# First chunk's gate moved behind the second chunk's step two, q loaded ahead of w_mod and half of it asked for by GpSimd, in a kernel of FFT convolution and token mixer

## The chip, the cores and the metric

The kernel runs on one core of a Trainium2 chip. The metric is the device time of one execution in microseconds (us), the median of several runs. Beside the runs, one execution was recorded by the profiler; its trace gives start and length of each instruction on the five engines: PE (TensorE matmul; PEld is its weight load), DVE (VectorE), ACT (ScalarE), POOL (GpSimd) and SP (SyncE, which here only asks for DMA transfers). A queue that asks for transfers is marked SPq or ACTq.

## The reference

Sequence 2048 (S), channels 640 (D), hidden size 1728 (F), all in float32:

```python
    mod = (_silu(c) @ w_mod).reshape(c.shape[0], 6, 1, -1)
    sa, ca, ga, sb, cb, gb = (mod[:, 0], mod[:, 1], mod[:, 2], mod[:, 3], mod[:, 4], mod[:, 5])
    h = _layernorm(x, axis=-1) * (1 + ca) + sa
    x = x + ga * _A_ref(h, A_k, A_v, A_shift_k, A_ssm_k, A_ssm_D)
    h = _layernorm(x, axis=-1) * (1 + cb) + sb
    x = x + gb * _B_ref(h, B_w1, B_b1, B_w2, B_b2)
```

with x = q at the start. `_A_ref` shifts k by a causal filter of four taps per channel, multiplies it by v (kv), convolves kv along the sequence with `ssm_k` per channel (by FFT), adds kv times `ssm_D`, and multiplies the result by h: the gate. `_B_ref` is an MLP over the sequence axis: layer norm, w1, gelu, w2. So h, the left factor of the gate, needs the layer norm of all of q and three of the six rows of mod; the convolution needs neither.

## The kernel before

The part that the change touches is the first block, `_A_ref`. It goes over five chunks of 128 channels (`NC = 5`, loop over `c` at L511). A chunk's convolution is a DFT in two steps each way, all of it matmuls on PE:

- kv (`kv_ops`, L171): four groups `g` of eight operations on DVE, or on POOL (its own scratch), from KX and VX (k and v of the chunk, in the tile `in`) into X, the tile `x`. The taps come from `rows` into TAP (PSUM) or PW.
- `ssm_k` is loaded into KSR, the lower half of the tile `aux` (`load_ks`, L149); POOL or DVE adds `ssm_D` (`perm_add`), ACT rearranges it into KSP, the tile `p` (`perm`).
- step one (`step1(side, t)`, L210): four blocks for X (side 0), four for KSP (side 1), each 16 matmuls into a PSUM buffer, evacuated by ACT into Z.
- step two (`f2(g)`, L223): eight blocks; 32 matmuls, ACT copies one half into kt, DVE multiplies twice into `p` (`mul`), POOL or DVE adds into `y` (`add`). `mul` of block g needs the half of `p` that `add` of block g - 2 has read.
- the way back (`i2`, L254, two halves; `i1`, L273, two halves): `i2` takes two PSUM buffers each, `i1` one.
- the gate (`gate`, L299): DVE multiplies A1 by the PSUM of `i1`, POOL adds the product to q in `xa` or `xb`; `spill` writes the chunk to DRAM. A1 is the upper half of `aux`: 16 rows of the normalized q by ACT (`a1_ops`, L286), times G1 and plus G0 by DVE.

PSUM has a ring of three buffers for all these steps and a fourth, `tap`, for taps and the sums of mod. The order is written by hand (the program is emitted in the order in which the engines run it); each engine goes through its instructions in that order, and so does each queue of DMA requests. While chunk c goes through step two, the kv work of a later chunk fills DVE's gaps (`fill`, taken by `dv(n)`).

The start and the first pass differ from the others. Chunk 0's kv is made before the loop, then chunk 1's, into the same X once PE has read it. SP's queue then holds w2 (the constants of step two), four bias loads into `g`, taps of chunk 2, q in 32 transfers of 64 rows (L494 to L496: for each of 16 `j`, the lower and the upper 64 partitions), and four of five parts of w_mod, two of which lie in the place of v1 (the constants of the way back) and two in `aux`. The mod rows come from five `mod_part`s on PE into `tap` (L338), `mod_sum`, and three `mod_row`s, which make G0 and G1 with ACT and DVE (L349).

In pass 0, after step two: 16 rows of statistics of q on DVE (L540 to L543), step one of chunk 1's kv, the `mod_part`s among `i2`, v1 and chunk 1's `ssm_k` only once parts of w_mod have been used, `rstd`, A1, chunk 2's kv group 2 on POOL, then `i1`, the gate of chunk 0, and step one of chunk 1's `ssm_k`. Then pass 1 begins with step two.

## Time and profile before

| what | value |
|---|---|
| runs | 696.41, 697.76, 707.59 us; median 697.76 |
| the profiled execution | 697.86 us, its span 696.1 us |
| mean granted PE clock | 0.975 of full |
| PE busy | 622.0 us, 89% of the span |
| DVE, ACT, POOL busy | 496.1, 291.6, 128.2 us |
| moved by DMA | 84.37 MB, 121 GB/s over the span |
| step two of chunks 1, 2, 3 begins on PE | 115.45, 164.87, 209.23 us |

The span runs from the first to the last instruction; what the time has beyond it lies around the program. The profile's page lists busy time by engine, the span in 40 slices, the DMA queues, the chain of work that ended last (followed back from the end, at each step to what released it), and the costliest groups of instructions. The timeline gives start and length of single instructions or runs of them, with the idle time before in brackets and what ended it. Names of tiles stand as out<-in; L59 is the line of the helper TT, so DVE's and POOL's elementwise work is told apart by its tiles. The times of an issue on SPq are those of the request, not of the data.

### The profile page before, as it was taken

To read this page: it belongs to the slowest core of one execution; us is meant where nothing else is said; L and a number is where in the kernel's file an instruction comes from. 1 tells how busy PE (TensorE), PEld (TensorE's weight loads), DVE (VectorE), ACT (ScalarE), POOL (GpSimd) and SP (SyncE) were. 2 spreads that over 40 slices of the span, in tenths; PEclk is the share of its full clock that TensorE was granted. 3 is DMA by queue.
4 is the path that set the end of the run, shared out by engine and by line. 5 is a ranking of instruction groups with operands and counts; after the bars stand their busy time and mean duration, and the time that the engine had idled before them with its cause. 6 is when DMAs were issued, how large, how long until landed. Compare 5 with 4: busy or idle time off the path is not lost.

```text
span 696.1 us, 20691 instructions
## 1 busy us (share of the span) xinstructions
PE 622.0 (89%) x9099; PEld 595.8 (86%) x9099; DVE 496.1 (71%) x866; ACT 291.6 (42%) x464; POOL 128.2 (18%) x147
## 2 busy tenths in 40 slices
PE   0689777898998988888899999999999989999997
PEld 0688466788988888778899979999999989999997
DVE  6769448978979449888985741123499868888986
ACT  0444373554746536456666232232244233233331
POOL 5184018513425025000100000000000430000000
PEclk9999798999999999999999999999999999999999
DMA  9988988627443424171305604433353533466611
GB/s 183 243 227 232 381 169 178 145 43 155 91 79 111 145 64 121 59 153 32 60 1 91 121 2 99 84 61 64 110 141 104 167 121 99 121 173 172 167 44 38
DMA packets 166930, 84.37 MB, mean 121 GB/s; under 512 B 91030, under 2 KB 157368, under 8 KB 166840
## 3 DMA queue, kind: packets, MB, share of 16 engines
q1 hardware_dynamic: 162292, 81.74, 46.9%
q10 hardware_dynamic: 4548, 1.31, 1.1%
q8 instruction: 71, 1.16, 0.7%
q14 instruction: 19, 0.16, 0.1%
HBM read 72.55 MB, written 10.49 MB: 119 GB/s over the span
## 4 chain that ended last, share of the span: by engine, by line
PE 62%; DVE 17%; DMA 6%; ACT 5%; SPq 4%; issue 3%; POOL 1%; ACTq 0%; POOLq 0%; DVEq 0%
PE pst L436 20%; PE pst L997 17%; PE pst L1074 7%; PE pst L218 5%; PE pst L233 4%; PE pst L262 4%; SPq L496 3%; DVE tap L59 3%; PE pst L282 2%; DVE p L59 2%; DMA aux<-in_A_ssm_k_dram 2%; DVE kt L59 2%; DMA w<-in_const_w_dram 1%; DMA aux<-in_w_mod_dram 1%; DVE aux L59 1%
## 5 line engine op out<-in xcount | busy, mean ns | idle before, releaser
L233 PE MATMUL pst<-z,w 128*64 128x64 f32 x2560 | 79.0, 223 | 12.0 <-ACT z L220 5.7
L233 PEld LDWEIGHTS pst<-z,w 128*64 128x64 f32 x2560 | 76.8, 138 | 14.8 <-issue 7.7
L220 ACT ACTIVATE z<-pst 128x1024 f32<-128x1024 f32 x40 | 43.0, 1076 | 51.4 <-PE pst L218 51.3
L218 PE MATMUL pst<-v,x 128*64 128x128 f32 x640 | 39.6, 282 | 27.2 <-DVE x L59 24.1
L218 PEld LDWEIGHTS pst<-v,x 128*64 128x64 f32 x640 | 36.9, 142 | 28.1 <-POOL t L459 23.6
L59 DVE TENSOR_TENSOR p<-pst,kt 128x512 f32<-128x512 f32 x80 | 50.9, 680 | 12.7 <-ACT kt L237 9.3
L59 POOL TENSOR_TENSOR y<-p 128x256 f32<-128x256 f32 x72 | 51.1, 744 | 38.8 <-DVE p L59 38.6
L218 PE MATMUL pst<-v,p 128*64 128x128 f32 x640 | 39.7, 283 | 6.8 <-DVE aux L59 4.6
L997 PE MATMUL pst<-r_z,m_w 128*128 128x320 f32 x222 | 42.1, 312 | 2.2 <-DVE m_w L59 2.2
L218 PEld LDWEIGHTS pst<-v,p 128*64 128x64 f32 x640 | 37.2, 143 | 8.0 <-DVE aux L59 4.9
L262 PEld LDWEIGHTS pst<-v,y 32*128 32x128 f32 x1280 | 39.7, 194 | 3.8 <-issue 2.6
L237 ACT ACTIVATE kt<-pst 128x512 f32<-128x512 f32 x40 | 23.9, 599 | 43.7 <-PE pst L233 30.1
L262 PE MATMUL pst<-v,y 32*128 32x64 f32 x1280 | 41.6, 279 | 0.7 <-ACT z L220 0.6
L833 ACT ACTIVATE pst<-pst,sm 128x640 f32<-128x640 f32 x13 | 10.0, 767 | 75.8 <-PE pst L436 75.8
L985 ACT ACTIVATE m_w<-m_v 128x896 fp32r<-128x896 f32 x24 | 22.7, 951 | 37.0 <-PE pst L997 16.8
L997 PEld LDWEIGHTS pst<-r_z,m_w 128*128 128x128 f32 x222 | 35.2, 190 | 2.4 <-DVE m_w L59 2.4
L59 DVE TENSOR_TENSOR tap<-tap,kt 128x512 f32<-128x512 f32 x51 | 35.5, 696 | 1.3
L59 DVE TENSOR_TENSOR kt<-in,tap 128x512 f32<-128x512 f32 x51 | 34.9, 685 | 1.4
L59 POOL TENSOR_TENSOR m_p<-u_i,r_z 128x320 f32<-128x320 f32 x1 | 0.9, 882 | 183.4 <-issue 183.4
L271 ACT ACTIVATE z<-pst 128x512 f32<-128x512 f32 x38 | 20.9, 646 | 21.9 <-PE pst L262 21.9
L59 DVE TENSOR_TENSOR m_w<-m_v,m_w 128x896 fp32r<-128x896 f32 x24 | 27.9, 1164 | 2.4 <-ACT m_w L985 1.9
L436 PE MATMUL pst<-r_z,wb0b 128*128 128x320 f32 x180 | 28.2, 310 | 0.9 <-DVE u_x L59 0.9
(289 smaller groups left out, 1445.0 us busy)
## 6 DMA issues: line engine op xcount, KB each, us to landing
x<-in_B_w_dram SPq DMA_DIRECT2D x20, 512.0 KB
aux<-in_A_ssm_k_dram SPq DMA_DIRECT2D x10, 512.0 KB
in<-in_A_k_dram SPq DMA_DIRECT2D x36, 128.0 KB
in<-in_A_v_dram SPq DMA_DIRECT2D x36, 128.0 KB
m_x<-xs SPq DMA_DIRECT2D x28, 160.0 KB
out_dram<-m_x SPq DMA_DIRECT2D x28, 160.0 KB
w<-in_const_w_dram SPq DMA_DIRECT2D x2, 2048.0 KB
m_v<-in_B_w_dram SPq DMA_DIRECT2D x9, 448.0 KB
```

The costliest lines, as they stand in the source:

```text
L59: TT = lambda eng, o, a, b, op: eng.tensor_tensor(o, a, b, op=op)
L218: pe.matmul(ps[64 * ri:64 * ri + 64, o:o + 255:2], lhs, F1[:, 128 * ri:128 * ri + 128], start=True, stop=True)
L220: evac = lambda: act.activation(Z[:, side, t], ps.rearrange("p (a k e) -> p a k e", a=4, e=2), AF.Copy)
L233: pe.matmul(ps[64 * h:64 * h + 64, o:o + 64], W2[k1 // 32][:, 2 * (k1 % 32) + ri], rhs, start=True, stop=True)
L237: act.activation(kt.rearrange("p (m i) -> p m i", i=32), pv[:, :, 1], AF.Copy)
L262: pe.matmul(pp[qd // 2][:, o:o + 64], Y[p, ri, i:i + 2].rearrange("p i k -> p (i k)"), V2[p, 64 * ri:64 * ri + 64], start=ri == 0, stop=ri ...
L271: act.activation(o, i, AF.Copy)
L436: pe.matmul(ps[0:m, h, 0:320], w_.bitcast(F32R), r_[:, 320 * h:320 * h + 320].bitcast(F32R), start=first and i == 0, stop=last and i == 2)
L496: sync.dma_start(XH[j // 8][64 * b:64 * b + 64, j % 8], dram(q, (16 * b + j) * D, [[32 * D, 64], [1, D]]))
L985: act.activation(W[n][0].bitcast(F32R), A[p, w_], AF.Copy)
L997: pe.matmul(bank[n], w[:, i].bitcast(F32R), r.bitcast(F32R), start=i == 0 and k == 0, stop=i == 6 and k == 2)
L1074: pe.matmul(acc[s][:, h, 0:320], w[:, f_].bitcast(F32R), u[r + h].bitcast(F32R), start=f_ == 0 and k == 0, stop=f_ == NF - 1 and k == 2)
```

## The change

Chunk 0's gate leaves pass 0. What pass 0 holds now is what the convolutions need:

- Chunk 1's kv goes to X1, the upper half of `aux` (A1's place), so it needn't wait for PE to read X. `step1` gets the place as an argument.
- The bias loads move to ACT's queue, and the transposition of them with Silu to before pass 0.
- SP's queue after w2: chunk 1's `ssm_k`, taps, v1, then k and v of chunk 2, then 16 transfers of q's lower rows, then three parts of w_mod, two of them in `aux` and one in `in`. The 16 transfers of q's upper rows are asked for by POOL, behind its group of chunk 2's kv.
- Pass 0 after step two: chunk 2's kv (three groups on DVE, one on POOL) into X; step one of chunk 1 from X1; the way back of chunk 0, whose result ACT copies to Y0 (the place of VX); step one of chunk 1's `ssm_k`; then statistics of q's first eight rows.
- Pass 1: step two, with one row of q's statistics after each block, the roots in four portions (`q_root`, `q_newton`), the first normalized rows of chunk 0 and three `mod_part`s; then two further `mod_part`s, step one of chunk 2, `mod_sum` and the `mod_row`s; chunk 0's gate in four portions (`late`) among `i2`; chunk 1's A1 and gate; step one of chunk 2's `ssm_k`; loads of k and v of chunk 3 as their places come free.
- POOL's group of chunk 3's kv stands after both gate adds of chunk 1. From there on the order is that of before.

The core of the diff:

```diff
+    act.dma_start(stg[0:13, :], dram(b1, 0, [[128, 13], [1, 128]]))
...
-    run(kv_ops(2, pool))
-    run(kv_ops(0))
-    run(kv_ops(1))
+    run(kv_ops(2, pool, X1))
+    run(kv_ops(0, dve, X1))
+    run(kv_ops(1, dve, X1))
...
-    for j in range(16):
-        for b in range(2):
-            sync.dma_start(XH[j // 8][64 * b:64 * b + 64, j % 8], dram(q, (16 * b + j) * D, [[32 * D, 64], [1, D]]))
+    def load_q(b, eng):
+
+        for j in range(16):
+            eng.dma_start(XH[j // 8][64 * b:64 * b + 64, j % 8], dram(q, (16 * b + j) * D, [[32 * D, 64], [1, D]]))
...
+    Y0 = T_in[:, 2240:4288].rearrange("p (j d) -> p j d", j=16)
+
+    def late(n):
+
+        t = ((T_t, T_kt)[n // 2])[:, 512 * (n % 2):512 * (n % 2) + 512].rearrange("p (j d) -> p j d", j=4)
+        g = lambda G: G[:, None, 0:DC].to_broadcast([128, 4, DC])
+        x = XH[n // 2][:, 4 * (n % 2):4 * (n % 2) + 4, 0:DC]
+        ac = [lambda j=j: act.activation(t[:, j], XR(4 * n + j, 0, DC), AF.Identity, scale=rs1[:, 4 * n + j:4 * n + j + 1],
+                                         bias=nm1[:, 4 * n + j:4 * n + j + 1]) for j in range(4)]
+        return ac, [lambda: TT(dve, t, t, g(G1), ALU.mult), lambda: TT(dve, t, t, g(G0), ALU.add),
+                    lambda: TT(dve, t, t, Y0[:, 4 * n:4 * n + 4], ALU.mult), lambda: TT(pool, x, x, t, ALU.add)]
...
+    load_ks(1)
+    load_taps(2)
+    sync.dma_start(T_v1[:, 0:4096], c_v1, max_dma_last_dim=4096)
...
+            if c == 1:
+                q_stats(range(8 + g, 9 + g))
+                if g in (1, 2):
+                    q_newton(g - 1)
+                if g in (3, 4):
+                    run(late(g - 3)[0])
+                if g == 4:
+                    q_root(2)
+                if g == 5:
+                    q_newton(2)
+                if g > 4:
+                    mod_part(tap, g - 5, three(pl[g - 5]))
+                    if g > 5:
+                        mod_load(0, g - 3, pl[g - 3])
...
         if c == 0:
-            mod_load(0, 4, P[:, 0:1920])
...
+            for g in range(4):
+                load_k(2, g)
+                load_v(2, g)
+            load_q(0, sync)
...
+            step1(0, 1, False, X1)
+            run(kv_ops(1, pool))
+            load_q(1, pool)
+            for g in (0, 2, 3):
+                run(kv_ops(g))
+            i2(0)
+            step1(0, 2, False, X1)
+            perm(1)
+            i2(1)
+            step1(0, 3, False, X1)
+            for kk in range(3):
+                mod_load(0, kk, pl[kk])
...
             for t in range(4):
+                step1(1, t)
+            q_stats(range(4))
+            q_stats(range(4, 8))
+            for n in range(2):
+                q_root(n)
+            continue
+        elif c == 1:
+            q_root(3)
+            step1(0, 0)
+            mod_part(tap, 3, three(pl[3]))
+            load_ks(2)
+            step1(0, 1)
+            mod_part(tap, 4, three(pl[4]))
...
+            mod_sum(tap, P[:, 0:640])
             i2(0)
...
+            mod_row(2, P[:, 0:640])
+            run(late(2)[0] + ac[0:4])
+            step1(0, 2)
+            run(late(0)[1] + late(1)[1] + late(2)[1])
             i2(1)
...
+            run(late(3)[1])
+            run(ac[4:16])
+            run(po)
...
+            for half in range(2):
+                ps = i1(half)
+                gate(1, ps, half)
+            spill(1)
+            for t in range(4):
+                step1(1, t)
             run(kv_ops(2, pool))
...
+            dv(8)
+            continue
```

Three places show how instructions move on an engine. First DVE, at the end of chunk 0's step two (p<-pst are the products of its last two blocks, `sm` holds the statistics). Before, with the first rows of q behind it:

```order
L59 TENSOR_TENSOR p<-pst_612,kt 128x512 x2
L59 TENSOR_TENSOR x<-tap,in 128x8x32x2
L59 TENSOR_TENSOR p<-pst_651,kt 128x512 x2
L542 BN_STATS sm<-xa 128x6 x2
L543 BN_AGGR sm<-sm 128x2
```

And now, with the end of chunk 1's kv in `aux`, and the first of three groups of chunk 2's kv:

```order
L59 TENSOR_TENSOR p<-pst_585,kt 128x512 x2
L59 TENSOR_TENSOR aux<-tap,in 128x8x32x2
L59 TENSOR_TENSOR p<-pst_624,kt 128x512 x2
L59 TENSOR_TENSOR tap<-in,tap 128x512
L59 TENSOR_TENSOR kt<-in,tap 128x512
L59 TENSOR_TENSOR tap<-tap,kt 128x512
```

The statistics, 16 rows there before, moved behind 24 operations of kv, and only eight of them are left in this place.

Second POOL, from the end of that group of kv (t is its scratch, x its result) to the next step two (y<-p). Before, up to the gate adds of chunk 0:

```order
L59 TENSOR_TENSOR t<-t 128x512
L59 TENSOR_TENSOR x<-t,in 128x8x32x2
L59 TENSOR_TENSOR xa<-xa,aux 128x8x128
L59 TENSOR_TENSOR xb<-xb,aux 128x8x128
L59 TENSOR_TENSOR y<-p 128x8x32 x4
```

And now, with the requests for q's upper rows in that place:

```order
L59 TENSOR_TENSOR t<-t 128x512
L59 TENSOR_TENSOR x<-t,in 128x8x32x2
L498 DMA xa<-in_A_q_dram 64x640 x8
L498 DMA xb<-in_A_q_dram 64x640 x8
L59 TENSOR_TENSOR y<-p 128x8x32 x14
```

The gate adds are gone from here, and 16 requests stand between POOL's kv and its adds for chunk 1's step two.

Third POOL again, later, between step two of chunk 1 and that of chunk 2, where before (the same names as above) only two gate adds stood:

```order
L59 TENSOR_TENSOR y<-p 128x8x32 x10
L59 TENSOR_TENSOR xa<-xa,aux 128x8x128
L59 TENSOR_TENSOR xb<-xb,aux 128x8x128
L59 TENSOR_TENSOR y<-p 128x8x32 x4
L59 TENSOR_TENSOR aux<-aux,rows 1x64 x2
```

And now:

```order
L636 MEMSET in 1x192 x2
L59 TENSOR_TENSOR xa<-xa,t 128x4x128 x2
L59 TENSOR_TENSOR xb<-xb,kt 128x4x128 x2
L59 TENSOR_TENSOR aux<-aux,rows 1x64 x2
L662 TENSOR_SCALAR t<-rows 128x256
L59 TENSOR_TENSOR xa<-xa,aux 128x8x128
L59 TENSOR_TENSOR xb<-xb,aux 128x8x128
L59 TENSOR_TENSOR t<-in,t 128x512 x2
```

Chunk 0's four gate adds and both of chunk 1 come here, and POOL's group of chunk 3's kv (its first row is the last shown) begins behind them.

More of the change, by code (lines that the diff above doesn't have):

```diff
@@ L207, in kv, with step1 @@
         return ops
-    def step1(side, t, later=False):
+    def step1(side, t, later=False, src=X):
         ps = psum()
@@ L506, in dv @@
+    three = lambda t: [t[:, 640 * j:640 * j + 640] for j in range(3)]
+    pl = [t[:, 0:1920] for t in (X1, KSR, T_in, KSR, T_in)]
+    load_ks(1)
+    load_taps(2)
+    sync.dma_start(T_v1[:, 0:4096], c_v1, max_dma_last_dim=4096)
+    ps = psum()
+    pe.transpose(ps[:, 0:36], stg, ID[0:36, 0:36])
+    act.activation(cols, ps[:, 0:36], AF.Copy)
+    act.activation(sil, cols[:, 30:35], AF.Silu)
+    fill = kv_ops(3, dve, X1)
     def dv(n):
@@ L538, in mixer_kernel @@
         pa_next(dve if c else pool)
-        if c == 0:
-            for j in range(16):
-                for h in range(2):
-                    dve.bn_stats(bst[:, j, h, :], XR(j, 320 * h, 320))
-                dve.bn_aggr(mv[:, j, :], bst[:, j, 0:2, :])
-        if c and c + 2 < NC:
+        if c > 1 and c + 2 < NC:
             taps()
@@ L637, in mixer_kernel @@
             ps = i1(half)
-            if c and half:
+            if half:
                 dv(3)
-            elif c:
+            else:
                 k0 = step1(1, 0, True)
-            elif half:
-                run(po[2:4])
             gate(c, ps, half)
         spill(c)
-        if c:
-            k0()
-        for t in range(1 if c else 0, 4):
+        k0()
+        for t in range(1, 4):
             step1(1, t)
```

107 lines of the change are left out of this document (55 added, 52 removed).

## The prediction

> **What bounds the kernel now.** I read the table of engines on the profile's page first, then the busy times of three stretches, cut where PE begins step two (the matmuls of `f2`) of chunks 1, 2 and 3; each row has the length, the busy time of PE, PEld, DVE, ACT and POOL, the granted clock, the DMA share and GB/s:
>
> ```profile
> PE 622.0 (89%) x9099; PEld 595.8 (86%) x9099; DVE 496.1 (71%) x866; ACT 291.6 (42%) x464; POOL 128.2 (18%) x147
> ...
> 58.46:115.45 56.99, 42.18 (x841) 34.35 (x841) 36.21 (x75) 26.78 (x43) 16.72 (x14) 0.82 0.92 249
> 115.45:164.87 49.42, 43.06 (x1280) 40.98 (x1281) 40.71 (x58) 26.17 (x42) 18.16 (x20) 1.00 0.53 112
> 164.87:209.23 44.36, 42.77 (x1281) 40.99 (x1281) 39.09 (x55) 26.11 (x42) 15.40 (x18) 1.00 0.48 101
> ```
>
> Over the whole run PE is 89% busy, and the later two stretches are full: 43.06 of 49.42 us, 42.77 of 44.36. The first is not: 42.18 of 56.99 us, at a clock of 0.82, while DMA moves 249 GB/s. PE's idle time in the three is 14.8 + 6.4 + 1.6 = 22.8 us; that bounds what another order of this work can bring, 3% of the run. Next the chain of waits, which says what PE stood behind in the first stretch (start, length, what):
>
> ```profile
> 70.18 9.66 DMA aux<-in_w_mod_dram
> ...
> 81.91 15.10 DMA aux<-in_A_ssm_k_dram
> ...
> 99.41 3.19 ACT aux L289 x8
> 102.62 2.22 DVE aux L59
> 104.86 2.18 DVE aux L59
> 107.14 1.24 DVE aux L59
> 108.42 5.90 PE pst L218 x64
> 114.34 1.07 ACT z L220
> 115.45 2.11 PE pst L233 x64
> ```
>
> First w_mod, which SP asks for after all of q; then chunk 1's `ssm_k`, asked for after w_mod; then the first gate's work on A1 by ACT and DVE. The gate holds the PSUM buffers that step one of chunk 1 needs next, so the chain comes back to PE only at 108.42. The timelines of the single engines give the durations below.
>
> **The change, part by part.** I work on the profiled run: its span is 696.1, its time 697.86, so 1.76 lie around the span. The median of the runs is 697.76, 0.1 less; the difference is not used.
>
> *To the end of chunk 0's step two: nothing.*
>
> ```profile
> 21.00 1.28 ACT L163 ACT_TABLE_LOAD   x1 [21.00 <-DMA aux<-in_A_ssm_k_dram]
> 32.74 0.69 DVE L59 TENSOR_TENSOR x<-tap,in 128x512 f32<-128x512 f32 x1 [2.57 <-PE pst L218]
> 37.78 2.52 POOL L59 TENSOR_TENSOR t<-in,t 128x512 f32<-128x512 f32 x2 [15.18 <-DMA in<-in_A_v_dram]
> 37.52 0.47 SPq L478 DMA_DIRECT2D g<-in_B_b_dram  x1
> 58.46 7.21 PE L218 MATMUL pst<-v,x 128*64 128x128 f32 x128 [0.55 <-DVE x L59]
> ```
>
> The four bias loads (on SP, the first at 37.52) go to ACT's queue, where ACT waits for `ssm_k` until 21.00 in any case. The transpose, its copy and Silu come ahead of step two, under 0.3 us on PE. Writing X1 and not X spares DVE its 2.57 us of waiting for PE at 32.74, but POOL's group, which waits for v until 37.78, and w2 are no earlier. Step one of chunk 1 begins at 58.46 as before.
>
> *From there to chunk 1's step two: 28 us less.*
>
> ```profile
> 6.06 0.69 DVE L59 TENSOR_TENSOR tap<-in,tap 128x512 f32<-128x512 f32 x1 [1.21 <-DMA in<-in_A_k_dram]
> 11.15 0.69 DVE L59 TENSOR_TENSOR x<-tap,in 128x512 f32<-128x512 f32 x1
> 59.91 0.88 DVE L542 BATCH_NORM_STATS2 sm<-xa 128x6 f32<-128x320 f32 x2
> 75.83 0.21 DVE L543 BATCH_NORM_AGGREGATE sm<-sm 128x2 f32<-128x12 f32 x1
> 36.85 9.74 DMA w<-in_const_w_dram
> 180.78 3.71 PE L218 MATMUL pst<-v,x 128*64 128x128 f32 x64
> 209.23 7.68 PE L233 MATMUL pst<-z,w 128*64 128x64 f32 x256 [1.15 <-ACT z L220]
> 8.43 2.49 POOL L59 TENSOR_TENSOR t<-in,t 128x512 f32<-128x512 f32 x2 [3.03 <-DMA in<-in_A_k_dram]
> 17.73 1.27 POOL L59 TENSOR_TENSOR x<-t,in 128x512 f32<-128x512 f32 x1
> L496 SPq DMA_DIRECT2D xa<-in_A_q_dram x16: 466/596/1426, 41.2 to 56.9; - x16
> ```
>
> PE has the steps that it has between chunks 2 and 3, from 180.78 to 209.23: 28.45 us, so step two could start at 58.46 + 28.45 = 87. DVE now does three groups of chunk 2's k and v, 24 operations 0.727 us apart (6.06 to 11.15 are seven steps), 17.4 us, then the statistics of eight rows, 1.01 us each (sixteen took from 59.91 to 76.04). They wait for data: behind w2 (landed at 46.59) SP's queue now holds 1 MB of `ssm_k`, 2 MB of v1 and 2 MB of k and v. At 249 GB/s the first group, 3.5 MB on, is there at 60.6, and the last by 67; I put 69, since its place is free only when DVE's work for chunk 1 ends, at 58. So DVE ends k and v at 78 and the statistics at 86.5, and the first product can start at 90, with PE's first block (2.11) and its copy (0.6) behind 87.5.
>
> The statistics need q's upper rows, for which POOL asks after its group 1: 10.6 us (8.43 to 19.0), from 64 to 74.6. No row prices a DMA issue on POOL. The nearest is the same load issued by SP, 0.596 us at the median, 1.426 at most. POOL takes 1.27 us where DVE takes 0.69, so I scale it: 0.596 x 1.27 / 0.69 = 1.1 us, and keep 0.6 (SP's own) and 2.6 (1.426 scaled alike) as ends. At 1.1 the sixteen end at 92.2 and the first eight have landed by 86: hidden, and at 0.6 as well. At 2.6 it costs 20 us (first rival). SP meanwhile holds the w_mod loads until PE frees X1 (about 74) and DVE and POOL free KX (78); behind them stand only chunk 2's `ssm_k` and chunk 3's k, not due before 137.
>
> A rule of the Trainium skill speaks against this part (SBUF — State Buffer, section SBUF: two separate sides, the box on DVE blocking DMA): while DVE runs an operation in a two-port mode, GpSimd is locked out and can't write descriptors. If it held for all of DVE's k and v work, POOL would start at 78, the sixteen would end at 95.6, and the sum would be the same; the same page of the Trainium skill gives tensor_tensor no two-port mode. No run here shows either yet.
>
> *Chunk 1's step two and tail: 14.4 us more.*
>
> ```profile
> 133.03 3.67 DVE L59 TENSOR_TENSOR p<-pst,kt 128x512 f32<-128x512 f32 x6
> 76.42 0.25 DVE L317 RECIPROCAL sm<-sm 128x16 f32<-128x16 f32 x1 [0.38 <-ACT sm L326]
> 184.43 3.80 PE L262 MATMUL pst<-v,y 32*128 32x64 f32 x128
> 188.26 2.23 ACT L271 ACTIVATE z<-pst 128x512 f32<-128x512 f32 x4 [0.71 <-PE pst L262]
> 91.56 0.70 ACT L360 ACTIVATE g<-pst 128x640 f32<-128x640 f32 x1
> 92.30 1.55 DVE L59 TENSOR_TENSOR g<-pst,g 128x640 f32<-128x640 f32 x2 [14.37 <-ACT g L360]
> 83.12 1.65 ACT L289 ACTIVATE aux<-xa,sm 128x128 f32<-128x128 f32 x4 [6.73 <-PE tap L342]
> 142.54 4.61 DVE L59 TENSOR_TENSOR aux<-aux,g 128x2048 f32<-128x2048 f32 x2
> ```
>
> Between the products on DVE now stand the statistics of eight rows and three root chains (1.5 us each, from 76.42 on): 8 x 1.22 + 8 x 1.01 + 3 x 1.5 = 22.3 us, more than PE's 8 x 2.11 = 16.9. The first statistics come before 90, so the products end at 112, the last adds at 113. Then what was moved here makes a chain that nothing covers: w_mod parts 3 and 4 on PE to 114.5 (part 4's place is free only after part 2, so its load of 4 to 5 us just fits); `i2(0)` 3.8, its evacuation 2.2, G0 and G1 1.4, DVE's products with G 1.55 (they free the PSUM that `i2(1)` needs), `i2(1)` 3.8, evacuation 2.2, late(3) 1.65, z 1.07, twelve rows of A1 4.95, A1's two products 4.6, two gates 2.5. That is 29.7, to 144.2. From the last gate to step two it was 115.45 - 108.38 = 7.1, so chunk 2's step two starts at 151.3, 63.8 us after chunk 1's, which was 49.42.
>
> *Chunk 2's step two: 5.2 us more.*
>
> ```profile
> 113.54 2.37 POOL L59 TENSOR_TENSOR xa<-xa,aux 128x1024 f32<-128x1024 f32 x1
> 118.99 1.43 POOL L59 TENSOR_TENSOR y<-p 128x256 f32<-128x256 f32 x2 [0.76 <-DVE p L59]
> 181.79 1.29 DVE L59 TENSOR_TENSOR p<-pst,kt 128x512 f32<-128x512 f32 x2 [0.58 <-ACT kt L237]
> ```
>
> POOL now does the two gate adds (143 to 147.8) before group 2 (10.6, to 158.4), and the first add of step two ends at 159.9. The third product needs its buffer and is ready at 159.4: 0.5 us. DVE has eight products and 16 operations of k and v, 2.7 us a block: the third ends at 161.2, the eighth at 174.7. From there to chunk 3 it took 209.23 - 183.08 = 26.15: 200.9, so 49.55 us and not 44.36.
>
> Sum: -27.95 + 14.38 + 5.19 = -8.4. Behind it the order is the same. Span 687.7, time 689.5; I say 690.
>
> **The rivals.** *POOL's issues are dear* (slower). With x us each, they end at 74.6 + 16 x, and step two's first add, behind them on POOL, 1.4 later. Chunk 1's third product needs it and is ready at 97.5, so x decides from 1.35 on. At 1.87 the gain is gone; from 2.74 the run is slower by 2% (712). For it: POOL's 1.8 to 1 against DVE, and SP's own 1.426. Against: an issue moves no data through POOL. By the Trainium skill (DMA: Bandwidth & Descriptors, Specifications) the first byte takes about 1 us on GpSimd's path and 0.6 on the others; by that, too, the sum stays at 690.
>
> *The transfers come no sooner.* The bytes are the same, and DMA's share was 0.92. If `ssm_k` takes its 15.10 us and not 4.2 (1 MB at 249 GB/s), then k, v, q and DVE come 10.9 later: 700, no change. Against: those 15.10 lay behind v1, and 3 MB of w_mod now come afterwards.
>
> *The tail packs better.* If A1's rows on ACT and the G chain fit under `i2`, 9 of the 19.6 us given back don't arise: 681. The bound of 22.8 allows 675.
>
> **Chances and range.** Mine 0.48, dear issues 0.20, transfers 0.18, packed tail 0.14; 690 is the likeliest. Mine alone runs from 685 to 696. With the transfers, issues up to 2.35 us (706) and the packed tail down to 679 the range holds 8 in 10. Within 2% (684 to 712, about what a measurement of this kernel can tell from no change) lie mine, the transfers and issues up to 2.74: 0.80. Faster by over 2% is the packed tail, 0.13; slower the dearest issues, 0.07.
>
> **What would show it.** PE's step two of chunks 1, 2 and 3 at 87.5, 151 and 201: the first tells of the transfers, the second of the tail, the third of POOL's order. POOL's rows of q: if they end past 96 and DVE's p waits for POOL in chunk 1, the issues are dear. The sum is wrong if chunk 1 starts after 95, or chunk 2 before 145.

## The result, and the profile after

The changed kernel takes 706.06 us at the median of 20 runs (703.47 to 715.98), the kernel before 700.59 in 20 runs taken beside them (695.67 to 707.59). The ratio is 1.0085, its 95% interval 1.0065 to 1.0105: a little slower, where 690 us was forecast, and 0.06 us beyond the range. Here and below, the ratios leave out executions in which the whole core ran slower (such as the one of 715.98 us), the medians hold them all. The profiled execution took 703.47 us with a span of 701.7 (before 697.86 and 696.1), so both traces lie about 2.7 us below the medians, and the spans differ by 5.6 us as the medians do.

The windows of the changed kernel, cut where chunk 0's step two ended before (58.46) and where step two of chunks 1, 2 and 3 now begins; columns as in the prediction's first fence:

```profile
58.46:96.35 37.89, 30.17 (x806) 28.34 (x806) 27.26 (x55) 18.21 (x22) 21.92 (x30) 0.95 0.96 218
96.35:162.71 66.36, 56.93 (x1352) 48.64 (x1352) 45.37 (x88) 35.98 (x66) 24.96 (x27) 0.90 0.64 157
162.71:215.12 52.41, 44.19 (x1281) 42.31 (x1281) 41.70 (x59) 26.24 (x42) 23.14 (x25) 0.97 0.45 95
```

Step two begins at 96.35, 162.71 and 215.12 us; the forecast was 87.5, 151.3 and 200.9, before it was 115.45, 164.87 and 209.23. So 19.1 of the 28 us are there at chunk 1, 2.2 are left at chunk 2, and at chunk 3 the kernel is 5.9 late, all that the span shows. In the first row PE is busy 30.17 of 37.89 us while DMA's share is 0.96. What it waits for stands in PE's waits from 58.46 to 115.45 (what waited, for what, us in total, times, longest):

```profile
PE pst L235 <- issue: 5.2, 3, 2.8
PE pst L284 <- issue: 4.9, 2, 4.4
...
PE pst L220 <- issue: 0.4, 1, 0.4
PE pst L264 <- issue: 0.3, 1, 0.3
```

10.8 us are put down to "issue": the engine waited for nothing that the profile shows. In the same window before, that was 0.4. The timeline of PE shows where:

```profile
59.13 1.32 PE L235 MATMUL pst<-z,w 128*64 128x64 f32 x37 [2.78 <-issue]
...
78.75 2.09 PE L284 MATMUL pst<-z,v 64*64 64x64 f32 x128 [0.49 <-issue]
85.22 1.35 PE L284 MATMUL pst<-z,v 64*64 64x64 f32 x41 [4.38 <-issue]
...
100.62 3.95 PE L235 MATMUL pst<-z,w 128*64 128x64 f32 x128 [1.49 <-issue]
105.46 5.17 PE L235 MATMUL pst<-z,w 128*64 128x64 f32 x169 [0.89 <-issue]
```

PE stops in the middle of loops: between two matmuls of one block of `i1`, with operands long there, it stands still for 4.38 us. From one stop to the next it is 128 matmuls or a multiple of that (in the rows that begin with a stop, 128 and 128; the 41 of `i1` and 87 of step one behind them make 128 again). Three windows around stops, where the DMA engines are full, and one with idle engines:

```profile
56.00:58.00 2.00, 0.35 (x11) 0.21 (x7) 2.00 (x4) 0.27 (x1) 1.55 (x4) 1.00 1.03 418
80.00:84.00 4.00, 0.84 (x59) 0.71 (x49) 3.90 (x10) 0.88 (x1) 2.41 (x5) 1.00 1.05 261
98.00:102.00 4.00, 2.51 (x86) 2.37 (x83) 2.68 (x9) 0.60 (x1) 1.42 (x2) 1.00 1.04 396
106.00:110.00 4.00, 4.00 (x144) 4.00 (x141) 3.73 (x9) 3.02 (x8) 2.03 (x3) 1.00 0.04 10
```

At a share of 1.03 to 1.05 there are stops, at 0.04 none. From the page, a line on DMA queues (packets, MB, share) says what may lie behind it; the line of the chain that ended last follows:

```profile
q8 instruction: 71, 1.16, 0.7%
...
PE 69%; DVE 15%; ACT 5%; issue 5%; POOL 3%; DMA 1%; SPq 0%; ACTq 0%; POOLq 0%; DVEq 0%
```

The queue of kind "instruction" moves 1.16 MB in 71 packets, so 16 KB each. PE has 9,099 matmuls and as many weight loads; 18,198 over 71 is 256 to a packet, which is 128 matmuls with their loads. (That this queue is PE's is read from this count; a second queue of that kind moves 0.16 MB.) The chain's share of "issue" went from 3% to 5%.

One more wait of PE was in no term of the sum, at the start of step one of chunk 3:

```profile
184.74 4.99 PE L220 MATMUL pst<-v,x 128*64 128x128 f32 x64 [4.29 <-DVE x L59]
```

It is for the last kv operation on DVE, 4.29 us. Last, what the first rival spoke of, POOL's requests for q, on POOL's timeline:

```profile
76.52 4.34 POOL L498 DMA_DIRECT2D xa<-in_A_q_dram  x8
```

Eight took 4.34 us, 0.54 each. By the view of q's tile their data land 8.1 us after the request at the median:

```profile
DMA to landing us min/median/max: 4.6/8.1/8.5
```

An issue is cheap, then, but its data stand in a long line. The line also holds up POOL: it asks for eight without a pause, and before seven of the other eight it waits until earlier rows have landed, 4.4 us in all, so that the sixteen take from 76.52 to 89.6, 0.82 us each. (The ninth is asked for at 81.36, 4.84 after the first; the quickest of POOL's rows landed 4.6 after its request.)

### The profile page after: what moved, and what is told of

The parts are those of the page before. It is cut to its first block, busy times and chain, and to the rows that moved or that the text cites. A ratio compares the mean times of both kernels' runs of the same rounds, so it can differ in the third digit from the quotient of the medians.

```text
span 701.7 us, 20783 instructions
## 1 busy us (share of the span) xinstructions
PE 624.7 (89%) x9099; PEld 597.8 (85%) x9099; DVE 494.7 (71%) x881; ACT 293.8 (42%) x469; POOL 148.0 (21%) x177
## 3 DMA queue, kind: packets, MB, share of 16 engines
q8 instruction: 71, 1.16, 0.7%
## 4 chain that ended last, share of the span: by engine, by line
PE 69%; DVE 15%; ACT 5%; issue 5%; POOL 3%; DMA 1%; SPq 0%; ACTq 0%; POOLq 0%; DVEq 0%
PE pst L438 19%; PE pst L1078 17%; PE pst L220 9%; PE pst L1155 7%; PE pst L235 6%; PE pst L264 6%; PE pst L284 2%; DVE tap L59 2%; DVE p L59 2%; PE tap L344 2%; DVE kt L59 1%; DVE aux L59 1%; ACT z L273 1%; PE pst L951 1%; POOL t L59 1%
## 5 line engine op out<-in xcount | busy, mean ns | idle before, releaser
L235 PEld LDWEIGHTS pst<-z,w 128*64 128x64 f32 x2560 | 76.6, 138 | 19.5 <-issue 11.9
L222 ACT ACTIVATE z<-pst 128x1024 f32<-128x1024 f32 x40 | 42.9, 1073 | 45.1 <-PE pst L220 45.1
L220 PE MATMUL pst<-v,x 128*64 128x128 f32 x512 | 36.3, 307 | 27.7 <-DVE x L59 27.7
L220 PEld LDWEIGHTS pst<-v,x 128*64 128x64 f32 x512 | 33.7, 158 | 30.1 <-POOL t L465 23.4
L59 DVE TENSOR_TENSOR tap<-tap,kt 128x512 f32<-128x512 f32 x48 | 33.4, 696 | 1.2
L59 DVE TENSOR_TENSOR kt<-in,tap 128x512 f32<-128x512 f32 x48 | 32.9, 686 | 1.5
L284 PEld LDWEIGHTS pst<-z,v 64*64 64x64 f32 x1280 | 21.6, 143 | 10.1 <-issue 6.2
L284 PE MATMUL pst<-z,v 64*64 64x64 f32 x1280 | 23.1, 228 | 7.9 <-issue 5.1
```

Source lines behind the costliest of these rows:

```text
L59: TT = lambda eng, o, a, b, op: eng.tensor_tensor(o, a, b, op=op)
L220: pe.matmul(ps[64 * ri:64 * ri + 64, o:o + 255:2], lhs, F1[:, 128 * ri:128 * ri + 128], start=True, stop=True)
L222: evac = lambda: act.activation(Z[:, side, t], ps.rearrange("p (a k e) -> p a k e", a=4, e=2), AF.Copy)
L235: pe.matmul(ps[64 * h:64 * h + 64, o:o + 64], W2[k1 // 32][:, 2 * (k1 % 32) + ri], rhs, start=True, stop=True)
L284: pe.matmul(ps[64 * b:64 * b + 64, 512 * e + 64 * jj:512 * e + 64 * jj + 64], V1[p, ri, n2], T2[p, :, 32 * ri + n2], start=ri == 0, stop=r ...
```

## The experiments

**Theories.** F: PE's instructions come in blocks of 128 matmuls through the same DMA engines as the data; a block has to wait behind data that has been asked for already, so PE stops where the engines are full. Before, PE stood waiting for data in that stretch anyway, and its blocks were there in time. R, a rival: POOL's queue as a second source of requests does it, not the amount of data. W, a second rival: the stops are waits of another kind that the profile doesn't name, and DMA being full is coincidence. Besides these, the late x on DVE was taken to come from the pace at which kv work is spread over step two. Where nothing else is said, the diff is against the changed kernel. "Before" in brackets is the median of the kernel before, run beside it on the same chip; not all experiments ran on one chip, so ratios are what is compared.

**q by SP alone.** What R calls for: the same bytes, without POOL.

```diff
-            load_q(1, pool)
+            load_q(1, sync)
```

> The changed kernel with q's upper rows asked for by SP behind the lower ones, as POOL's part undone. Theory F: PE's instructions come through the same DMA engines in blocks of 256 (128 matmuls with their weight loads), and PE stops where a block comes late because the engines are full; the bytes are the same here, so the stop of 4.38 us in the second i1 of pass 0 stays between 2 and 5 us, and the run between 700 and 709. Rival R: it is POOL's queue, as one more queue on the engines, that keeps the blocks waiting; then the stop falls under 1 us, and step two of chunk 1 begins before 93 unless q's upper rows now come later. Rival W: PE waits there for a transfer or an engine that the profile doesn't name; then the stop stays as it is, at 4.4.

704.87 us (8 runs; before 700.14), ratio 1.0068 (1.0032 to 1.0105). The stop in `i1` is 2.48 us; step two of chunk 1 begins at 91.83, but q's upper rows now come after all lower ones, and PE waits 2.85 us for DVE's products behind the statistics:

```profile
82.75 0.81 PE L284 MATMUL pst<-z,v 64*64 64x64 f32 x41 [2.48 <-issue]
...
100.50 2.72 PE L235 MATMUL pst<-z,w 128*64 128x64 f32 x64 [2.85 <-DVE p L59]
```

Stops stay without POOL, so R falls as the cause of all of it; whether a second queue adds to them isn't settled, and as a measure of size this run says less than it seems, as the next shows.

**The pace of the fill.** Chunk 2's step two takes the kv operations in six blocks again, as before.

```diff
-            dv(-(-len(fill) // max((6 if c > 2 else 8) - g, 1)))
+            dv(-(-len(fill) // max((6 if c > 1 else 8) - g, 1)))
```

> The changed kernel with the kv work in chunk 2's step two spread over six blocks and not eight. In the changed kernel step one of chunk 3 waits 4.29 us for DVE's last kv operation. If that wait is a term of the loss, it goes below 1 us and the run gains 2 to 4 us against the changed kernel, 702 to 704 at a changed kernel of 706. Rival: DVE has no slack in this stretch, the operations only change places and the products come later by as much; then the wait turns into one of PE for DVE's p, and the time stays within 1 us.

700.43 us (10 runs; before 700.14), ratio 1.0006 (0.9974 to 1.0039): this line alone is worth the whole loss, and more than the 2 to 4 us expected of it. From the timeline of PE, a stop in chunk 1's step two, then the row at the start of step one of chunk 3:

```profile
103.00 7.82 PE L235 MATMUL pst<-z,w 128*64 128x64 f32 x169 [4.18 <-issue]
...
181.15 3.86 PE L220 MATMUL pst<-v,x 128*64 128x128 f32 x64 [0.44 <-DVE p L59]
```

The wait of 4.29 us is 0.44, and from chunk 2's step two to chunk 3's it takes 209.72 - 162.14 = 47.6 us, not 52.4. Up to 160 us this kernel has the same instructions as the changed one, yet its stops are others: 1.27 us in `i1` and 4.18 here. Chunk 1's step two begins at 90.95 and not at 96.35, but chunk 2's at 162.14, only 0.57 us sooner: the later stop, and the slower clock behind it, took back what the shorter one had left. So a single stop in a single trace scatters by several us; what follows rests on the ratios of many runs, with the traces to show the place.

**Copies in the kernel before.** 5.2 MB from DRAM to DRAM, read by nothing, asked for by POOL ahead of chunk 2's step two, where the kernel before has no stops (diff against the kernel before; its lines lie one further on):

```diff
+        if c == 1:
+            for i in range(8):
+                pool.dma_start(xs2[256 * i:256 * i + 256, :], dram(q, 256 * i * D, [[D, 256], [1, D]]))
```

> The kernel before, with eight copies of 640 KB from DRAM to DRAM (q to a scratch tensor that nothing reads) asked for by POOL after chunk 1's gate adds, so that they move while PE is in chunk 2's step two, which has no stop of PE without a named wait now. Nothing waits for the copies. Theory F: PE then stops there between blocks of 128 matmuls, for 2 us or more in all, each stop marked as issue. Rival W: no such stop, PE's step two of chunk 2 takes 16.1 us as before, or waits only for named engines.

One execution: 709.55 us. PE in that step two, first before, then with the copies:

```profile
164.87 16.13 PE L233 MATMUL pst<-z,w 128*64 128x64 f32 x512 [1.15 <-ACT z L220]
```

```profile
166.93 4.18 PE L234 MATMUL pst<-z,w 128*64 128x64 f32 x136 [1.15 <-ACT z L221]
174.81 5.44 PE L234 MATMUL pst<-z,w 128*64 128x64 f32 x127 [3.70 <-issue]
184.18 9.81 PE L234 MATMUL pst<-z,w 128*64 128x64 f32 x249 [3.92 <-issue]
```

512 matmuls ran through in 16.13 us; with the copies they stop twice, for 3.70 and 3.92 us, behind 136 and a further 127 matmuls. Windows of the same kernel:

```profile
172.00:176.00 4.00, 1.19 (x37) 1.18 (x38) 3.31 (x6) 0.29 (x1) 2.84 (x5) 0.97 1.06 340
180.00:184.00 4.00, 0.26 (x10) 0.17 (x5) 1.90 (x3) 1.36 (x3) 1.76 (x3) 0.82 0.69 237
184.00:188.00 4.00, 3.82 (x73) 3.82 (x74) 0.00 (x0) 0.47 (x1) 0.00 (x0) 0.50 0.89 209
```

The engines are full around the first stop (1.06, with 340 GB/s) and from 176 to 180 (1.15, 336 GB/s); the second stop, 180.25 to 184.18, still runs on while the copies end (0.69). Nothing else was changed there, so the transfers make the stops and W falls; and since stops come without POOL's queue too, F is left. What the copies don't tell apart is the DMA engines and the memory that copies and instructions come from. The last window tells one thing more: behind this stop the granted clock is 0.50.

**Less of q.** 64 of 640 columns of each row are loaded, the rest of q is left out (the tiles are zeroed at the start by POOL).

```diff
-            eng.dma_start(XH[j // 8][64 * b:64 * b + 64, j % 8], dram(q, (16 * b + j) * D, [[32 * D, 64], [1, D]]))
+            eng.dma_start(XH[j // 8][64 * b:64 * b + 64, j % 8, 0:64], dram(q, (16 * b + j) * D, [[32 * D, 64], [1, 64]]))
```

> The changed kernel with only the first 64 of q's 640 columns loaded (0.5 MB in place of 5.2, as many requests and rows), the rest of the tiles set to zero by POOL while it waits for k; so the layer norm and the output are of other data. Theory F: with the engines free from about 72 us on, the stop of 4.38 us in i1 falls under 0.5 us, the stops from 60 to 115 us from 10.8 to under 3 us in all, and step two of chunk 1 begins at 89 to 92 and not at 96.35. Rival W: the stops stay, since PE's code, w2 and v1 are the same.

One execution: 697.04 us; the stop in `i1` 0.98 (under 0.5 was expected), chunk 1's step two at 89.60. A stop of 2.26 us is left in that step two (96.11 to 98.37), behind w_mod's transfers at 398 GB/s from 92 to 96. The same with the fill over six blocks:

> The changed kernel with both cuts at once: the kv fill of chunk 2's step two over six blocks, and only 64 of q's 640 columns loaded (the tiles are zeroed by POOL at the start; the output is not the reference's). If PE's stops (theory F) and DVE's late x are two separate terms, they add: no 4.3 us wait for x, stops in i1 under 1.3, chunk 1's step two at 89 to 91, chunk 3's at 202 to 205, span 689 to 692. Rival 'one hides the other' (with x no longer late, chunk 2's step two is bound by POOL's y or DVE's products and nothing of q's cut arrives): chunk 3 at 207 or later, span 694 to 696.

691.55 us (4 runs; before 699.77), ratio 0.9886 (0.984 to 0.9931). The starts of step two:

```profile
89.32 6.51 PE L235 MATMUL pst<-z,w 128*64 128x64 f32 x215 [1.13 <-ACT z L222]
...
154.46 9.68 PE L235 MATMUL pst<-z,w 128*64 128x64 f32 x320 [1.16 <-ACT z L222]
...
202.32 7.69 PE L235 MATMUL pst<-z,w 128*64 128x64 f32 x256 [1.14 <-ACT z L222]
```

Both the starts and the stop in `i1` (0.97) are as expected. Against the run with the pace alone, taking 4.7 MB of q away is worth 1.2% of the time, some 8 us. The two terms add: the pace is worth 5.6 us with all of q (706.06 - 700.43) and 5.5 with a tenth (697.04 - 691.55, the first of these a single execution). In the traces it is 4.8 and 4.7: from chunk 2's step two to chunk 3's, 52.41 falls to 47.58, and 52.54 to 47.86. So with the fill's pace of before, the new order takes about the forecast 690 us when q's transfers don't stand in PE's way. It is no gain that could be had: the kernel before loads all of q, and this run doesn't.

**q in longer requests.** Four rows in one request, meant to make the packets four times as long, the same bytes (on top of the pace):

```diff
-        for j in range(16):
-            eng.dma_start(XH[j // 8][64 * b:64 * b + 64, j % 8], dram(q, (16 * b + j) * D, [[32 * D, 64], [1, D]]))
+        for j in range(0, 16, 4):
+            eng.dma_start(XH[j // 8][64 * b:64 * b + 64, j % 8:j % 8 + 4].rearrange("p j d -> p (j d)"),
+                          dram(q, (16 * b + j) * D, [[32 * D, 64], [1, 4 * D]]), max_dma_last_dim=2560)
```

> The changed kernel with the kv fill of chunk 2's step two spread over six blocks again (as in the run with the fill's pace), and q asked for in four requests per half, four rows of j in each, so that its packets are 10 KB and not 2.5 KB; the bytes are the same. If PE's blocks of instructions come late because q's many short packets keep the DMA engines full (theory F), q's bytes should move at the 350 to 420 GB/s that w_mod and v1 showed and not at 230 to 280: PE's stops put down to 'issue' between 58 and 100 us fall from 6.6 to 9.8 us to under 4, chunk 1's step two begins at 88 to 90, chunk 3's at 204 to 207, and the time is 693 to 697. Rival 'bytes decide': q takes as long as before, and one long packet ahead of PE's block costs it more than a short one: stops as long or longer, chunk 1 at 91 or later, the time 700 or more. Rival R (POOL's requests themselves): only 8 requests fewer of 0.5 us each, no change within 1 us.

706.39 us (12 runs; before 699.77), ratio 1.0084 (1.0049 to 1.012). I expected a gain and got a loss of 6 us against the run with the pace alone; the rival 'bytes decide' had the outcome right (chunk 1's step two at 91 or later, here 97.39, and 700 us or more). PE in `i1`:

```profile
86.25 1.35 PE L284 MATMUL pst<-z,v 64*64 64x64 f32 x41 [7.69 <-issue]
```

It stands for 7.69 us, the longest stop of all. The windows there, the line on landing, and from 83.2 to 83.6 us the queue with SP's half of q (packets, MB, share):

```profile
80.00:84.00 4.00, 0.00 (x0) 0.00 (x0) 3.55 (x6) 0.00 (x0) 1.37 (x3) 0.78 1.08 203
84.00:88.00 4.00, 1.75 (x45) 1.63 (x46) 0.00 (x0) 0.34 (x1) 0.00 (x0) 0.50 1.04 234
```

```profile
DMA to landing us min/median/max: 11.6/17.4/22.2
...
q1 hardware_dynamic: 31, 0.08, 98.9%
```

The packets did not get longer: 0.08 MB in 31 is 2.6 KB each, one row of q, and from 74 to 100 us no data packet has 8 KB. So the run says nothing on the length of packets. What did change is that the requests are out sooner: all of q within 7 us (74.3 to 81.3; 71.2 to 89.6 in the changed kernel), since POOL with its four requests never waits for one to land, and POOL's data land 17.4 us after the request and not 8.1. The bytes flow no faster (203 and 234 GB/s). DVE's statistics wait 7.2 us for q here, but up to 125 us PE waits for DVE only once, 0.4 us ahead of step one, so its late start isn't DVE's doing. That is F in a sharper form: what counts is how much data has been asked for ahead of the block.

**The packets of instructions.** The records of the DMA queues show them one by one. In stretches of 0.4 us the queue of kind "instruction" is there in one of ten or more; this is its line for 82.4 to 82.8 us in the changed kernel, one packet, 0.02 MB:

```profile
q8 instruction: 1, 0.02, 19.6%
```

So read, around the stops of three kernels:

| kernel | packet moved between | PE goes on at |
|---|---|---|
| changed | 56.8 and 57.2 | 59.13 |
| changed | 82.4 and 82.8 | 85.22 |
| changed | 98.0 and 98.4 | 100.62 |
| changed | 102.8 and 103.2 | 105.46 |
| q in longer requests | 83.2 and 83.6 | 86.25 |
| q in longer requests | 100.0 and 100.4 | 102.75 |
| before with copies | 172.0 and 172.4 | 174.81 |
| before with copies | 181.2 and 181.6 | 184.18 |

Each time PE goes on 1.9 to 3.1 us behind a packet, and in between no other packet comes. Where PE doesn't stop they come every 4.4 to 4.8 us (61.6, 66.4, 70.8, 75.6 in the changed kernel). That is F seen directly, but for one thing: the records have no time at which a packet was asked for. The packet itself is about half of the way: 19.6% of 16 engines over 0.4 us is 1.25 us of one engine. The distances also tell why `i1` is hit hardest: there 128 matmuls last 2.09 us, in step two 3.95, in step one about twice that (64 in 3.7). The block at 85.22 came 6.5 us after PE had taken up the one before (78.75), 4.4 more than that one lasted; with a tenth of q it was 3.1 (2.09 + 0.97).

**POOL's kv ahead of the gate adds.** The third term of the sum, on top of the pace:

```diff
+            run(kv_ops(2, pool))
             for half in range(2):
                 ps = i1(half)
                 gate(1, ps, half)
...
-            run(kv_ops(2, pool))
```

> The kernel with the fill over six blocks, and POOL's group of chunk 3's kv ahead of both gate adds of chunk 1, so that it can begin at about 149 and not at 159.5. Theory (third term of the prediction: the products of chunk 2's step two wait for POOL's y because the kv group stands before it): POOL's first y comes at 165 to 167 and not 170, PE's waits for DVE's p in chunk 2's step two (0.97, 1.17, 0.44, 0.44 us) fall by 1 to 2 us, the time by 1 to 2. Rival: the gate adds then end at 164 and not 159.5, and ACT's rows of A1 for chunk 2, which write what they read, hold up ACT's copies into kt: step two's first products come 2 to 3 us later, and the time is the same or up to 2 us longer.

701.97 us (12 runs; before 699.77), ratio 1.0029 (1.0003 to 1.0056), no better than the run with the pace alone. POOL's first add comes at 167.33 instead of 170.09, yet PE's waits in chunk 2's step two are the same to 0.01 us (0.98, 1.16, 0.44, 0.44). With the fill over six blocks, DVE's products set the pace there, one every 3.26 us at first, and DVE waits for POOL in neither trace. Nor did ACT lose what the rival feared: its first copy into kt begins 2.13 us after the start of step two in both.

**Less asked for at a time.** Three steps, each on top of the one before. First q by SP alone, row by row, both halves one behind the other:

```diff
-    def load_q(b, eng):
+    def load_q(eng):
...
+            for b in range(2):
+                eng.dma_start(XH[j // 8][64 * b:64 * b + 64, j % 8], dram(q, (16 * b + j) * D, [[32 * D, 64], [1, D]]))
...
-            load_q(0, sync)
+            load_q(sync)
...
-            load_q(1, pool)
```

> The changed kernel with the fill of chunk 2's step two over six blocks, and all 32 requests of q by SP, row after row of j with both halves one behind the other (the order of the kernel before), none by POOL. Theory F in its sharper form, that PE's block of instructions stands behind all the data already asked for (the stop was 7.69 us when all of q was asked for within 6.6 us by 8 long requests, 4.38 with both queues asking, 2.48 with SP alone): SP alone asks for 0.16 MB per 0.6 us, about what the DMA engines move, so little stands ahead. The stop in i1 is 1 to 2.5 us; unlike the run with SP alone, the first rows are there with both halves early, so DVE's products aren't late; chunk 1's step two begins at 88.5 to 91, chunk 3's at 205 to 208, and the time is 0.992 to 0.998 of the kernel before. Rival 'w_mod and the rest': SP now ends q later (95) and w_mod's 3 MB come in the middle of step two: what the first stop gives back the next one, at 98 to 106 us, takes, and the time is 0.999 to 1.005.

697.74 us (12 runs; before 699.00), ratio 0.9979 (0.9951 to 1.0007). The time was as expected and the stop in `i1` too (1.76 us), the places weren't: chunk 1's step two begins at 92.29, behind a stop of 3.06 us in chunk 0's, and chunk 3's at 210.40 (205 to 208 was expected). Then two of the three first parts of w_mod by POOL, behind blocks of step two:

```diff
                 if g in (3, 4):
                     run(late(g - 3)[0])
+                    mod_load(0, g - 2, pl[g - 2], pool)
...
-            for kk in range(3):
+            for kk in range(1):
```

> The run with q by rows from SP, and besides only the first of the three parts of w_mod asked for at once; the second and the third are asked for by POOL after blocks 3 and 4 of chunk 1's step two, so that less data stands ahead of PE's blocks of instructions there. Theory F: the stop that the w_mod lump brings in step two (4.18 us at 98.8, with the granted clock at 0.50 to 0.73 for 6 us behind it) shrinks to under 2; the later part of step two and its tail begin 2 to 3 us sooner; the time is 2 to 3 us under the run without this edit, 0.988 to 0.995 of the kernel before. Rival 'only moved': the same bytes keep the DMA engines full later, the stop comes at 104 to 112 and is as long, or PE waits for w_mod itself (its parts are due at about 105, 108 and 111); no difference to the run without it within 1 us, or slower.

696.88 us (12 runs; before 699.00), ratio 0.996 (0.993 to 0.999). The median is 0.9 us lower, less than the 2 to 3 expected; the trace has no stop in chunk 1's step two, but one ahead of it, in chunk 0's, while v1 is loaded. So last v1 in four portions:

```diff
-    sync.dma_start(T_v1[:, 0:4096], c_v1, max_dma_last_dim=4096)
...
                 load_v(2, g)
+                sync.dma_start(T_v1[:, 1024 * g:1024 * g + 1024], c_v1[:, 1024 * g:1024 * g + 1024], max_dma_last_dim=4096)
```

> The run with two parts of w_mod by blocks, and besides v1 (2 MB, first used by the way back's second half at 78 us) no longer in one request ahead of chunk 2's k and v but in four of 0.5 MB, one behind each group of k and v. Theory F: the stop of 3.06 us at 56.8 to 59.9, which fell while v1's lump kept the DMA engines at 360 to 422 GB/s, shrinks to under 1; step one of chunk 1 begins at 58.5 to 60 and not at 62, chunk 1's step two at 89.5 to 91 and not 92.6; the time is 1 to 3 us under the run without this edit, 0.990 to 0.995 of the kernel before. Rival 'only moved': the stop comes in the 64 to 80 us that were full at seven to eight tenths, or v1's last part is late for the way back at 78; no difference within 1 us, or slower.

693.95 us (7 runs; before 697.94), ratio 0.9945 (0.9917 to 0.9972), faster than both kernels. The timeline of PE and the windows there, without the last edit:

```profile
59.90 2.29 PE L235 MATMUL pst<-z,w 128*64 128x64 f32 x37 [3.06 <-issue]
```

```profile
56.00:58.00 2.00, 0.84 (x29) 0.70 (x23) 2.00 (x4) 0.60 (x1) 1.56 (x3) 1.00 1.04 422
58.00:60.00 2.00, 0.10 (x2) 0.11 (x4) 0.73 (x2) 0.00 (x0) 1.03 (x2) 0.81 1.05 360
60.00:62.00 2.00, 2.00 (x39) 2.00 (x41) 0.00 (x0) 0.00 (x0) 0.00 (x0) 0.50 1.39 191
```

PE stops at 422 and 360 GB/s, and goes on at half the clock. The same two views with the edit:

```profile
58.75 3.71 PE L220 MATMUL pst<-v,aux 128*64 128x128 f32 x64 [0.62 <-DVE aux L59]
...
82.48 0.81 PE L284 MATMUL pst<-z,v 64*64 64x64 f32 x41 [2.19 <-issue]
...
91.55 9.70 PE L235 MATMUL pst<-z,w 128*64 128x64 f32 x320 [1.12 <-ACT z L222]
```

```profile
56.00:58.00 2.00, 1.96 (x62) 1.81 (x57) 2.00 (x5) 0.60 (x1) 1.56 (x3) 1.00 0.74 229
58.00:60.00 2.00, 1.38 (x27) 1.28 (x25) 1.69 (x4) 1.13 (x2) 1.22 (x3) 1.00 0.97 236
```

The stop of 3.06 us is gone with the 422 GB/s; step one of chunk 1 begins at 58.75, as was forecast. A stop of 2.19 in `i1` stays (and one of 1.87 ahead of it), and chunk 1's step two begins at 91.55, not by 91. Of the three steps none is beyond doubt by itself, since neighbouring intervals overlap; the first and the last of the row are just apart: 1.0006 (0.9974 to 1.0039) with the pace alone, 0.9945 (0.9917 to 0.9972) with all. The bytes are the same in both.

All stops of PE between 45 and 113 us, added up from each trace, and the start of chunk 2's step two in the same trace, beside the ratio of the runs:

| kernel | stops, us | chunk 2's step two, us | ratio to before |
|---|---|---|---|
| before | 1.6 | 164.87 | 1 |
| changed | 12.0 | 162.71 | 1.0085 |
| q by SP alone | 6.7 | 162.15 | 1.0068 |
| fill's pace | 7.8 | 162.14 | 1.0006 |
| pace, POOL's kv first | 8.6 | 163.21 | 1.0029 |
| pace, q in longer requests | 13.6 | 166.64 | 1.0084 |
| pace, q by rows | 8.0 | 162.52 | 0.9979 |
| and w_mod by blocks | 6.4 | 157.12 | 0.996 |
| and v1 in portions | 5.9 | 156.06 | 0.9945 |
| pace, a tenth of q | 4.9 | 154.46 | 0.9886 |

The changed kernel, the pace and POOL's kv have the same instructions up to 113 us: 7.8 to 12.0 is the scatter of one trace. Where chunk 2's step two begins scatters less in these three, 162.14 to 163.21, and the last two steps stand clear of that. (The traces of q by SP alone and of q by rows are of executions 2.6 and 2.7 us above their medians, all others of executions 1.9 to 4.4 below; before and changed 2.7 and 2.6 below.)

## Why the prediction was wrong

From 200.9 to 215.12 at chunk 3 it is 14.2 us, in three terms: 8.85 up to chunk 1, 2.6 more up to chunk 2, 2.9 more up to chunk 3. With them the time of 689.5 becomes 703.7; the trace's execution took 703.47. How the first two share their 11.4 is chance: in the traces with the pace and with POOL's kv first, which have the same instructions there, chunk 1's step two began at 90.95 and 97.01 and chunk 2's at 162.14 and 163.21, so the sum of the two was 10.8 and 11.9.

**"To the end of chunk 0's step two: nothing."** Not so: step one of chunk 1 begins at 60.3 and not at 58.46, behind the stop of 2.78 us. The stop is worth about half of that: with the pace, whose trace has none there, it began at 59.44, since PE waited 1.96 us for DVE's last operation on X1. The transfers that the change puts into SP's queue behind w2 (`ssm_k`, v1) were counted for when their data are due, not for what stands behind them.

**"From there to chunk 1's step two: 28 us less."** This is the step that failed. It took PE's 28.45 us from a stretch where DMA's share was 0.48 and put it into one where the prediction itself had DMA all but full (0.92), as if only data could be late there. The trace has 36.0 us from 60.3 to 96.35, 5.5 of them stops, and behind the longest a granted clock of 0.75 and 0.50 (84 to 86 and 86 to 88 us). With a tenth of q it took 29.6 (59.73 to 89.32). What was argued about DVE and POOL held to within 4 us: DVE did chunk 2's kv from 63.2 to 81.2 (78 was forecast) and the eight statistics to 90.4 (86.5), which was just in time for a product at 90, and PE, not DVE, was late.

Requests on POOL took 0.54 us where they followed one another, below the lower end of the range that I gave (0.6), and 0.82 with the waits for landing, which the forecast didn't have; they ended at 89.6. The rival of dear issues, which decides from 1.35 us on, is out. So is the wait of chunk 1's products for POOL: POOL waited for them, 10.36 us before its first add. The rule of the Trainium skill by which DVE can hold up GpSimd's requests (SBUF — State Buffer, SBUF: two separate sides) changed nothing: POOL issued eight requests in 4.34 us while DVE was busy with kv for 3.79 of the 4 us up to 80, which agrees with that page's giving tensor_tensor no two-port mode.

The rival of the late transfers came nearest, with chunk 1 at 98 and 700 us, but by another mechanism: it had DVE waiting for k and v, and in the trace DVE waits 7.56 us for kt, and so for PE.

**"Chunk 1's step two and tail: 14.4 us more."** It is 16.9 more (66.36 us). Two stops in step two make 1.49 + 0.89 = 2.4 of the 2.6 missing. The rest only came out even, by luck: DVE's products end 23.5 us after the start (forecast 24.5, which has no stops), and the tail behind them is 42.9 (39.3). The way back begins 4.7 us behind the products and not 2.5, since blocks of step one of chunk 2, 1.97 us each, stand between the w_mod parts, which the chain left out; the mod rows on PE add another 1.2:

```profile
118.56 1.29 DVE L59 TENSOR_TENSOR p<-pst,kt 128x512 f32<-128x512 f32 x2
```

That is the last product; on PE's timeline, the two blocks:

```profile
118.21 1.97 PE L220 MATMUL pst<-v,x 128*64 128x128 f32 x32
...
121.42 1.97 PE L220 MATMUL pst<-v,x 128*64 128x128 f32 x32
```

They begin behind the third and the fourth part. The first runs while DVE is still at its last product; the second is the one that lengthens the chain.

**"Chunk 2's step two: 5.2 us more."** It was 8.0. The sum counted DVE's load (2.7 us a block) and POOL's order, and not what comes next on PE: step one of chunk 3, which needs the last of the kv operations. Spread over eight blocks that operation ends at 184.6, just ahead of the eighth product, and PE is through with step two at 180.4. With the fill over six blocks the term is 3.2 (47.6 - 44.36), less than forecast, and POOL's order isn't part of it. In the changed kernel it is a small one: DVE waits 1.16 us for POOL's y once.

So the order as such can give what was forecast: 0.9886 with a tenth of q and the pace of before, at 691.55 us. Of the 16 us between 690 and 706.06, the line of the diff on the fill's pace costs 5.6, as much as the whole loss, and q's transfers 8 to 9 (700.43 against 691.55). That the latter act through the fetch of PE's instructions is shown by the packets and the copies; that no other part of it goes another way isn't shown. What stays open is where a packet waits, in the line of one of the sixteen engines, ahead of all, or in memory, and what PE does in the 1 to 2 us between the end of its packet and its next matmul; no run took that apart.

## What to carry to other kernels

A duration taken from a stretch where the DMA engines had room (28.45 us at a share of 0.48) need not hold where they are full (36.0 us at 0.95), even if every operand is there: PE's code, a packet for every 128 matmuls, comes as late as data does. Look for "issue" pieces at even distances in a dense loop, and then ask for less at a time, so that no long line of transfers is outstanding when the loop runs. And when filler work is spread thinner, look who waits for its last piece.

## What was not expected of the hardware

PE's instructions come in packets of 16 KB, 256 instructions each, and wait in line with data: the stop in `i1` was 1.27 to 5.32 us (three traces) with q at 0.16 MB a request and 7.69 (one trace) with 0.64 MB. The Trainium skill (Runtime: NRT & Kernel Launch, Instruction fetch mechanics) has the 16 KiB blocks and says that the cost of crossing into the next is mostly hidden; the packets agree, and hidden it is only while the DMA engines have room: 16.13 us for 512 matmuls before, some 27 us with the copies (166.93 to 193.83).

A stop can cost twice. In the run with the pace, the granted clock was down behind one of 4.18 us:

```profile
100.00:104.00 4.00, 1.00 (x18) 1.01 (x20) 3.55 (x13) 0.00 (x0) 1.96 (x4) 0.73 1.04 353
104.00:108.00 4.00, 4.00 (x82) 4.00 (x80) 2.38 (x7) 2.13 (x5) 1.34 (x3) 0.50 0.90 340
```

At 0.50, PE did 82 matmuls in 4 us; those 169 (the 7.82 us above) took 5.17 in the changed kernel, so the clock made the stop 2.65 us longer. It isn't so behind each: after the 2.78 us that end at 59.13 in the changed kernel the clock stayed at 1.00.

q moved slower than w_mod and v1 in either form: 203 and 234 GB/s in four-row requests, 261 in the changed kernel's window from 80 to 84, against 396 and 418. No run took apart why.
